# One PSUM tile of two banks for both halves of batch 0's kv, and the first half divided in two VectorE operations for four

## Chip, cores, metric

One core of one Trainium2 chip. The metric is the device time of an execution in microseconds (us). A time is the median of several runs unless a mean is named. The profile shows one execution each; its span is about 1.8 us shorter than the time.

## The reference, cut to what matters

Linear attention for 8 batches of 8 heads, 576 rows of 64, then a two-layer MLP with GELU on the result:

```python
q_s = softmax(q, axis=-1);  k_s = softmax(k, axis=2)      # k over the sequence
kv  = einsum('bhsd,bhse->bhde', k_s, v)                   # 64 x 64 for each head
x   = einsum('bhsd,bhde->bhse', q_s, kv)
out = gelu(x @ w_in) @ w_out                              # 4608 x 512, d_ff 2048
```

The kernel leaves out the division of k's softmax. It multiplies exp(k) by v with a column of ones added (65 columns), and divides kv by its 65th column afterwards.

## The kernel before

The MLP takes nearly all of the time on TensorE (lines 348, 376 and 401: 255.3 of its 270.9 us busy in the profile). The change touches the start-up, in which batch 0 is prepared while TensorE has nothing else to do.

```python
def kv_tiles(b):
    if b == 0:      # first half: two tiles of one bank; second half: a tile of two banks
        p = [psum_h.tile([128, 512], FP32, tag="h", name="kv")[:, 0:256] for i in range(2)]
        ps = psum_a.tile([128, 4, 256], FP32, tag="a2", name="kv")
        st[b]["kvall"] = ps[:, 0::2]
        p += [ps[:, 0, :], ps[:, 2, :]]
    else:           # other batches: all four pairs in one tile of two banks
        ps = psum_a.tile([128, 4, 256], FP32, tag="a2", name="kv")
        st[b]["kvall"] = ps
        p = [ps[:, i, :] for i in place]
    st[b]["kv"] = p
place = [1, 2, 0, 3]

# ... in kv_norm, for each part (src in PSUM, dst in SBUF, m pairs of heads):
    nc.vector.reciprocal(rec[:, 0:m], src[:, :, D])
    nc.vector.tensor_tensor(out=dst, in0=src[:, :, 0:D],
        in1=rec[:, 0:m].unsqueeze(2).to_broadcast([128, m, D]), op=ALU.mult)

# ... the start-up, in program order:
exp_q(0, parts=2)
exp_k(0, parts=2)
norm_q(0, 0, 2)                  # multiply on GpSimd (POOL)
norm_q(0, 1, 2, nc.vector)       # multiply on VectorE (DVE)
tp_mm(0, 0)                      # transposes of q for x of pairs 0, 1
cast_v(0, 0, nc.scalar)
cast_v(0, 1, nc.scalar)
tp_evac(0, 0)
cast_v(0, 2, nc.gpsimd)
cast_v(0, 3, nc.gpsimd)
# ... x tiles
tp_mm(0, 1)                      # transposes of q for x of pairs 2, 3
tp_evac(0, 1, "s")
# ...
kv_mm(0, 0)                      # kv of pairs 0, 1
kv_norm(0, 0)                    # their division
kv_mm(0, 1)                      # kv of pairs 2, 3
kv_norm(0, 1)
# ... casts of w_in, x tile
x_mm(0, 0); x_evac(0, 0, "s"); x_evac(0, 1)
x_mm(0, 1); x_evac(0, 2, "s"); x_evac(0, 3)
# ... then h_phase(0): the MLP
```

The softmax here doesn't subtract the row's maximum and nothing guards it: scores larger than these inputs give would overflow.

## Time and profile before

| | before |
|---|---|
| time | 279.40 us (3 runs, 279.39 to 279.44) |
| span of the profile | 277.5 us |
| TensorE busy | 98% |
| first half's division | 4 VectorE operations, 0.76 us from first start to last end |
| first MLP matmul | 13.97 us |

The row to watch is the last one. From there on TensorE (PE) runs without waits (busy 260.1 of the 263.5 us from 14 us to the end), so the time is the start of the MLP plus a constant.

### The profile page before, as it was taken

The numbers are of one execution on the slowest core, as the hardware profiler recorded it, in microseconds if no ns is written. First come the engines' busy times: TensorE is split into PE (matmuls) and PEld (weight loads), VectorE is DVE, ScalarE is ACT, GpSimd is POOL, SyncE is SP. The second block draws the span as 40 slices with busy tenths as digits, with TensorE's granted clock in tenths as the row PEclk, the third lists the DMA queues.
The fourth block names the chain that finished last, engine by engine and source line by source line (L and its number), as shares of the span: only waits on it lengthen the run. The fifth ranks groups of instructions, "written<-read, shape, count | busy, mean of one in ns | idle before, by whom it ended". The sixth has DMA issues, their size and how long they took to land.

```text
span 277.5 us, 4658 instructions
## 1 busy us (share of the span) xinstructions
PE 270.9 (98%) x1966; PEld 125.6 (45%) x1966; DVE 100.8 (36%) x154; ACT 158.9 (57%) x247; POOL 32.5 (12%) x26
## 2 busy tenths in 40 slices
PE   7799999999999999999999999999999999999995
PEld 3344454444444444444444444444444444444443
DVE  2876565319743540263008400751015200120012
ACT  4867686689377717791669246943683363126400
POOL 1520041002020310013000500050005000000000
PEclk9999999999999999999999999999999999999999
DMA  7999999974993249613981189117402500220033
GB/s 258 400 374 427 402 400 404 400 271 116 312 307 64 77 109 297 239 40 94 268 320 38 53 215 398 56 41 193 109 0 78 151 0 0 78 76 0 2 76 77
DMA packets 44980, 50.10 MB, mean 181 GB/s; under 512 B 20384, under 2 KB 29856, under 8 KB 44704
## 3 DMA queue, kind: packets, MB, share of 16 engines
q1 hardware_dynamic: 44560, 49.39, 53.5%
q10 hardware_dynamic: 400, 0.43, 0.5%
q8 instruction: 15, 0.25, 0.4%
q14 instruction: 5, 0.04, 0.1%
HBM read 36.70 MB, written 9.44 MB: 166 GB/s over the span
## 4 chain that ended last, share of the span: by engine, by line
PE 94%; DMA 4%; POOL 0%; DVE 0%; issue 0%; SPq 0%
PE ps L348 44%; PE ps L376 44%; DMA f<-in_v_dram 2%; PE kv L206 2%; PE ps L315 2%; DMA f<-in_q_dram 2%; PE ps L401 1%; PE pair L348 1%; POOL v_aug L169 0%; PE ps L320 0%; PE tp L279 0%; SPq L103 0%; DVE kvc L225 0%; DVE y_sb L406 0%; DVE rec L224 0%
## 5 line engine op out<-in xcount | busy, mean ns | idle before, releaser
L348 PE MATMUL ps<-xT,wi_bf 128*128 128x512 bf16 x568 | 124.9, 379 | 0.0
L376 PE MATMUL ps<-wo_bf,g 128*128 128x512 bf16 x560 | 124.1, 379 | 0.0
L354 ACT ACTIVATE g<-ps 128x512 bf16<-128x512 f32 x142 | 83.5, 598 | 66.8 <-PE ps L348 66.7
L348 PEld LDWEIGHTS <-wi_bf 128*128 128x128 bf16 x576 | 56.2, 98 | 68.0 <-issue 0.8
L376 PEld LDWEIGHTS <-g 128*128 128x128 bf16 x560 | 54.0, 98 | 64.6 <-issue 0.4
L384 DVE COPY y_sb<-ps 128x512 f32<-128x512 f32 x33 | 22.7, 687 | 81.0 <-PE ps L376 80.7
L245 POOL TENSOR_TENSOR e<-e,recq 128x2048 bf16<-128x2048 bf16 (+1 forms) x9 | 25.7, 2855 | 175.9 <-DVE recq L244 141.2
L169 DVE CAST v_aug<-f 128x576 bf16<-128x576 f32 x24 | 16.4, 746 | 48.3 <-DMA f<-in_v_dram 48.3
L243 DVE TENSOR_REDUCE qsum<-e 128x16 f32<-128x1024 bf16 (+1 forms) x13 | 21.1, 1622 | 13.7 <-ACT e L152 13.6
L341 ACT CAST xT<-ps 128x512 bf16<-128x512 f32 x18 | 9.9, 588 | 26.4 <-PE ps L315 15.9
L152 ACT ACTIVATE e<-f 128x512 bf16<-128x512 f32 (+1 forms) x42 | 20.5, 556 | 3.5 <-DMA f<-in_q_dram 3.5
L157 ACT ACTIVATE ek<-f 128x2304 bf16<-128x2304 f32 (+1 forms) x10 | 17.2, 1728 | 0.6 <-DMA f<-in_k_dram 0.5
L339 DVE CAST xT<-ps 128x512 bf16<-128x512 f32 x17 | 11.0, 687 | 17.1 <-PE ps L315 14.1
L79 ACT ACT_TABLE_LOAD x9 | 11.5, 1283 | 2.8 <-issue 2.7
L494 PE MATMUL ps<-zeros 128*128 128x512 f32 x14 | 8.0, 734 | 1.5 <-DVE zeros L520 1.5
L152 ACT ACT_TABLE_LOAD x7 | 9.0, 1283 | 0.1
L453 DVE CAST wi_bf<-w 128x512 bf16<-128x512 f32 x12 | 7.1, 621 | 1.8 <-DMA w<-in_moe_w_in_dram 1.4
L206 PEld LDWEIGHTS <-ek 64*64 64x64 bf16 x576 | 6.4, 105 | 2.2 <-issue 0.6
L206 PE MATMUL kv<-v_aug,ek 64*64 64x65 bf16 x576 | 6.8, 193 | 0.5 <-POOL v_aug L169 0.5
L487 DVE CAST wo_bf<-w 128x2048 bf16<-128x2048 f32 (+1 forms) x5 | 4.5, 907 | 6.1 <-DMA w<-in_moe_w_out_dram 6.1
L245 DVE TENSOR_TENSOR e<-e,recq 128x1024 bf16<-128x1024 bf16 x4 | 6.2, 1544 | 0.1
L315 PE MATMUL ps<-qT,kvc 64*64 64x512 bf16 x62 | 5.4, 390 | 0.3 <-DVE kvc L225 0.3
(40 smaller groups left out, 48.2 us busy)
## 6 DMA issues: line engine op xcount, KB each, us to landing
out_dram<-y_sb SPq DMA_DIRECT2D x32, 256.0 KB, 2.4
f<-in_k_dram SPq DMA_DIRECT2D x6, 1152.0 KB, 9.9
f<-in_v_dram SPq DMA_DIRECT2D x6, 1152.0 KB, 11.7
f<-in_q_dram SPq DMA_DIRECT2D x6, 1024.0 KB, 7.7
w<-in_moe_w_in_dram SPq DMA_DIRECT2D x6, 512.0 KB, 8.6
f<-in_v_dram SPq DMA_DIRECT2D x8, 288.0 KB, 6.5
f<-in_q_dram SPq DMA_DIRECT2D x4, 512.0 KB, 8.9
w<-in_moe_w_out_dram SPq DMA_DIRECT2D x2, 1024.0 KB, 11.4
```

What stands on the lines that cost most here:

```text
L79: nc.scalar.activation(out=scr[:, 1:2], in_=scr[:, 0:1], func=func)
L152: nc.scalar.activation(out=dst[:, i], in_=src[:, u], func=AF.Exp)
L157: nc.scalar.activation(out=ek[b % 2][:, i:i + n], in_=st[b]["kf"][:, i:i + n].rearrange("p x (n d) -> p x n d", n=NS), func=AF.Exp,)
L169: eng.tensor_copy(out=o, in_=i)
L206: nc.tensor.matmul(st[b]["kv"][hp][c, 0:D + 1], ek[b % 2][pr, hp, n, :], v_aug[b % 2][pr, hp, n, 0:D + 1], start=(n == 0), stop=(n == NS - 1),
L243: nc.vector.reduce_sum(out=qsum, in_=eq[:, :, hs, :], axis=AX.X)
L245: eng.tensor_tensor(out=eq[:, :, hs, :], in0=eq[:, :, hs, :], in1=recq.unsqueeze(3).to_broadcast([128, J, w, D]), op=ALU.mult,)
L339: nc.vector.tensor_copy(out=st[b]["xT"][:, hp, :], in_=ps)
L348: nc.tensor.matmul(ps, wi_bf[:, dm, t * 128:(t + 1) * 128], st[c]["xT"][:, dm, :], start=(dm == 0), stop=(dm == NDM - 1),)
L354: nc.scalar.activation(out=st[c]["g"][:, t, :], in_=ps, func=AF.Gelu)
L376: nc.tensor.matmul(ps, st[c]["g"][:, t, j * 128:(j + 1) * 128], wo_bf[:, t, :], start=(t == 0), stop=(t == NDF - 1),)
L384: nc.vector.tensor_copy(out=y_sb, in_=ps)
```

## The change

Its intent is to treat batch 0 as the other batches are treated: kv of all four pairs in one PSUM tile of two banks. Pairs 0 and 1 then lie side by side, so that one reciprocal and one multiply divide both. Two VectorE operations fewer, and two PSUM buffers fewer taken.

```diff
     def kv_tiles(b):
-        if b == 0:
-            p = [psum_h.tile([128, 512], FP32, tag="h", name="kv")[:, 0:256] for i in range(2)]
-            ps = psum_a.tile([128, 4, 256], FP32, tag="a2", name="kv")
-            st[b]["kvall"] = ps[:, 0::2]
-            p += [ps[:, 0, :], ps[:, 2, :]]
-        else:
-            ps = psum_a.tile([128, 4, 256], FP32, tag="a2", name="kv")
-            st[b]["kvall"] = ps
-            p = [ps[:, i, :] for i in place]
-        st[b]["kv"] = p
+        ps = psum_a.tile([128, 4, 256], FP32, tag="a2", name="kv")
+        st[b]["kvall"] = ps
+        st[b]["kv"] = [ps[:, i, :] for i in place]
 ...
-        elif b == 0 and half == 0:
-            parts = [(st[b]["kv"][hp].unsqueeze(1), kvc[b][:, hp:hp + 1], 1) for hp in range(2)]
-        elif b == 0:
-            parts = [(ps, kvc[b][:, 2:4], 2)]
         else:
             parts = [(ps[:, 1:3] if half == 0 else ps[:, 0::3], kvc[b][:, 2 * half:2 * half + 2], 2)]
```

## The prediction

> **What bounds the kernel now.** I read the page's first part, then the waits of PE, then the chain that ended last, and at last the timeline of the two microseconds that the change touches.
>
> ```profile
> PE 270.9 (98%) x1966; PEld 125.6 (45%) x1966; DVE 100.8 (36%) x154; ACT 158.9 (57%) x247; POOL 32.5 (12%) x26
> ```
>
> TensorE (PE) is busy 98% of a span of 277.5 us; VectorE (DVE), whose instructions the change cuts from 154 to 152, only 36%. Busy is not proof, so who stops PE? The list of PE's waits, over the whole span:
>
> ```profile
> PE ps L494 <- DVE zeros L520: 1.5, 1, 1.5
> PE ps L259 <- DVE e L245: 0.6, 1, 0.6
> PE kv L206 <- POOL v_aug L169: 0.5, 1, 0.5
> PE ps L259 <- POOL e L245: 0.4, 1, 0.4
> PE ps L315 <- DVE kvc L225: 0.3, 1, 0.3
> ```
>
> Columns: who waited, for whom, us in total, times, longest. Asked again from 14 us on, the list holds only the last line (that wait began before 14). So after the start-up PE never waits by this view; anything that moves the start of the dense part moves the end, one for one. All that matters is what sets the moment, 13.97 us, at which the first MLP matmul (line 348) starts. The chain of waits between 10 and 16 us (start, length, what):
>
> ```profile
> 11.12 0.67 POOL v_aug L169
> 11.79 0.05 issue
> 11.83 0.68 POOL v_aug L169
> 12.51 0.04 issue
> 12.55 0.50 PE kv L206 x34
> 13.05 0.02 issue
> 13.08 0.18 DVE rec L224
> 13.26 0.02 issue
> 13.28 0.30 DVE kvc L225
> 13.58 0.04 issue
> 13.63 0.41 PE ps L315 x4
> ```
>
> This chain is of batch 0's **second** half: v arrives, GpSimd (POOL) casts two slices, PE makes kv of head pairs 2 and 3, DVE divides them (one reciprocal, one multiply), PE makes x of pairs 2 and 3. The four DVE operations of the **first** half, which the change merges, are not in it. The timeline shows them beside it:
>
> ```profile
> 12.08 0.17 DVE L224 RECIPROCAL rec<-kv 128x1 f32<-128x1 f32 x1 [0.61 <-PE kv L206]
> 12.28 0.23 DVE L225 TENSOR_TENSOR kvc<-kv,rec 128x64 bf16<-128x64 f32 x1
> 12.42 0.16 DVE L224 RECIPROCAL rec<-kv 128x1 f32<-128x1 f32 x1
> 12.55 0.47 PE L206 MATMUL kv<-v_aug,ek 64*64 64x65 bf16 x34 [0.50 <-POOL v_aug L169]
> 12.61 0.23 DVE L225 TENSOR_TENSOR kvc<-kv,rec 128x64 bf16<-128x64 f32 x1
> 13.08 0.17 DVE L224 RECIPROCAL rec<-kv 128x2 f32<-128x2 f32 x1 [0.24 <-PE kv L206]
> 13.28 0.29 DVE L225 TENSOR_TENSOR kvc<-kv,rec 128x128 bf16<-128x128 f32 x1
> ```
>
> PE starts kv of the second half at 12.55, in the middle of these four: today it does not wait for them, because they read other PSUM tiles than it writes. This is the point on which my prediction rests.
>
> [...] In the new tile of two banks, pair 0 lies in slot 1 and pair 2 in slot 0 of the same bank, pairs 1 and 3 in the other: the second half's matmuls write the banks that the first half's division reads. [...] The built program agrees: against the kernel before, PE's list has exactly one new wait, on VectorE at the first weight load of kv's second half, and lacks three: the two on VectorE ahead of the first x matmuls (now covered by the earlier one) and one on an earlier PE result. No other wait differs. [...]
>
> [...] 64 columns more take a multiply from 0.226 to 0.291 us (65 ns, about 1 ns a column), and a reciprocal of 2 columns takes 0.171 against 0.157 to 0.169 for 1. So merging pays on DVE; the question is only who waits.
>
> **The change part by part.** Starts below are of single records in the trace, in us.
>
> 1. DVE. Before: reciprocal 12.076, multiply 12.279, reciprocal 12.421, multiply 12.612, the last ends at 12.838; 0.762 from start to end. After: one reciprocal and one multiply of the forms that the second half shows (13.076, then 13.281 for 0.291: 0.496 from start to end). Saved on DVE: 0.762 - 0.496 = 0.27 us; the division ends at 12.076 + 0.496 = 12.572 instead of 12.838.
>
> 2. What this gain could free. Next in PE's queue behind kv's second half is x of pairs 0 and 1. PE works in order and issues its last kv matmul at 12.838; the x matmul of pair 0 went at 12.841, that of pair 1 at 12.893, because the division ended at 12.838 and a weight load follows its DVE signal after about 0.053 (12.838 to 12.891; again 13.572 to 13.624). So at most 0.05 us, and in x of the first half, whose only follower is an ACT copy of xT that ends at 13.924.
>
> 3. The new wait. kv's second half starts now 0.052 after the POOL cast (12.501 to 12.553). After: 12.572 + 0.053 = 12.625, when the cast is long ready. Cost: 12.625 - 12.553 = 0.072 us, on the chain. Two of its 36 matmuls, which went ahead at 11.86 before, now come after the wait. The 36 of the first half took 0.289 from first to last start (11.549 to 11.838) against 0.285 for the 34 (12.553 to 12.838): 0.004 more.
>
> 4. From there the chain moves as a whole: last kv matmul 12.914, reciprocal 0.238 later, multiply 0.205 later, x of pairs 2 and 3 0.343 after that: 13.70 instead of 13.626. DVE was free from 12.838 and idle 0.24 us before the second half's reciprocal, so its saved work helps nothing here.
>
> 5. The first MLP matmul, before at 13.974, had two things to meet: PE's own switch after the last x matmul (13.636 + 0.332, the gap that the same switch shows at 44.637 to 44.969) = 13.968, and xT of pair 0, ended at 13.924 plus 0.05 = 13.974. After: the first is 13.713 + 0.332 = 14.045; the second, with x of the first half starting about 12.917 without a wait for pair 1, ends its copy near 13.953, so 14.003. The larger sets it: 14.045 - 13.974 = **0.07 us later**.
>
> 6. PSUM buffers. The two tiles no longer taken from the three-buffer pool advance its rotation by two. x of pair 3 gets a fresh bank instead of one used by a transpose; the next MLP tiles still find one that was freed long ago. Worth: 0, as the list of waits says.
>
> 7. Downstream. Between 14 and 39.6 us no matmul starts more than 0.25 after the one before, so no cast or load now stops PE, and being later only adds slack. The larger gaps later (0.31 to 0.41, around 40 and 44 us, and one or two per batch) are switches of matrix shape and an ACT copy that PE itself releases; they move along. Nothing absorbs the 0.07.
>
> Sum: +0.07 us on 279.40, so **279.47 us**, +0.03%.
>
> **The rivals.**
> - *The division is on the path, and two operations fewer bring a gain.* For it: PE's list has a wait for kvc at line 315. Against it: the chain shows that this is the second half's division, which is already two operations. It could give 0.05 to 0.27: 279.1 to 279.35.
> - *The wait is hidden anyway*: if the division ended before the POOL cast, or if the shift met slack at 13.97. The margin is small: the cast is ready at 12.501 and the division at 12.572. A reciprocal starting 0.07 earlier, or v landing 0.07 later in a run, makes it 0: 279.40. Half hidden is quite possible[...].
> - *The wait costs more than I count*: the semaphore covers a later operation, or weight loads that ran ahead before the cast was ready now queue behind the wait. That would add about 0.1 (a weight load takes 0.103): 279.6. Against: at line 315 a load behind a DVE signal and its matmul start within 0.002.
> - *The shift pushes transfers*: the cast of wi part 1 on DVE (14.72) frees a staging buffer and moves 0.07 later; but the queue sets out one load every 0.6 us or more and PE has no wait on these data. 0.
>
> **Range and chances.** All mechanisms together lie within -0.3 and +0.2 us. The three runs of before span 0.05 us, but its profiled run took 279.26, so another session may move by about 0.15. Range 279.2 to 279.75. Two per cent is 5.6 us, more than the whole stage from 11.1 to 14: within 2% is all but certain, 0.98. What is left goes slightly more to slower[...]: 0.013, faster 0.007.
>
> **What would show it.** In the profile after: two DVE operations for the first half, 128x2 and 128x128, ending 0.50 after their start; kv's second half starting about 0.05 after that end with VectorE named in place of POOL, near 12.62; both x groups and the first line-348 matmul about 0.07 later; PE's total unchanged. Wrong would be: kv's second half still beginning before the division ends (then the wait is not what I read), POOL still named as its releaser, the first MLP matmul at 13.97 or earlier, or a time below 279.3 or above 279.7 in paired runs.

The sum came to +0.07 us on 279.40, so 279.47 us.

## The result, and the profile after

| | before | after |
|---|---|---|
| time | 279.39 us (6 runs, 279.25 to 279.44) | 279.62 us (6 runs, 279.54 to 279.76) |
| ratio of the fast runs | | 1.0009, interval 0.9997 to 1.0022 |
| span of the profile | 277.5 us | 277.9 us |
| VectorE busy, instructions | 100.8 us, 154 | 100.0 us, 152 |
| first MLP matmul | 13.97 us | 14.33 us |

A ratio is the mean time of one kernel's fast runs over that of the other's of the same rounds, so not quite the ratio of the medians quoted. Within 2%, as predicted. The interval even holds 1.0, but no run of after is as fast as any of before, and a second session (below) gave +0.21 us again, though there some runs of the two overlap. So I take the change to be slower by about 0.2 us.

The list of PE's waits after the change (who, for whom, us in total, times, longest):

```profile
PE ps L483 <- DVE zeros L509: 1.5, 1, 1.5
PE ps L248 <- POOL e L234: 0.7, 1, 0.7
PE kv L199 <- DVE kvc L214: 0.6, 1, 0.6
PE ps L248 <- DVE e L234: 0.5, 1, 0.5
PE ps L304 <- DVE kvc L214: 0.4, 1, 0.4
```

Behind the edit, line numbers are 7 or 11 lower. The third line is new: kv now waits for VectorE's kvc, where it waited for POOL's cast of v. The timeline of the same stage (start, length, engine, operation, and in brackets the idle time before it and what ended it):

```profile
10.97 1.37 POOL L169 CAST v_aug<-f 128x576 bf16<-128x576 f32 x2 [0.93 <-DMA f<-in_v_dram]
...
12.35 0.17 DVE L213 RECIPROCAL rec<-kv 128x2 f32<-128x2 f32 x1 [0.63 <-PE kv L199]
12.55 0.29 DVE L214 TENSOR_TENSOR kvc<-kv,rec 128x128 bf16<-128x128 f32 x1
12.89 0.37 PEld L199 LDWEIGHTS <-ek 64*64 64x64 bf16 x36 [0.73 <-DVE kvc L214]
12.90 0.48 PE L199 MATMUL kv<-v_aug,ek 64*64 64x65 bf16 x36 [0.61 <-DVE kvc L214]
```

The merged division works as meant: two operations, 0.50 us. But PE starts the second half only behind them, at 12.90, although POOL had v cast at 12.34. What now stands behind this moment is seen in the chain of waits:

```profile
9.40 1.73 DVE e L234
11.13 0.14 issue
11.27 0.61 PE ps L248 x8
11.87 0.45 PE kv L199 x36
12.32 0.02 issue
12.35 0.18 DVE rec L213
12.53 0.02 issue
12.55 0.30 DVE kvc L214
12.85 0.04 issue
12.90 0.52 PE kv L199 x35
```

Before, v's transfer and casts led to kv's second half. After, it is the q path: normalization, transposes, kv's first half, its division. In this run that path is also later than in the profile before (transposes at 11.27, not 11.01), for a reason that nothing in the change explains at once. Whether that is chance was the first question to test.

### The profile page after: what moved, and what is told of

The parts are those of the page before. It is cut to its first block, busy times and chain, and to the rows that moved or that the text cites. A ratio compares the mean times of both kernels' runs of the same rounds, so it can differ in the third digit from the quotient of the medians.

```text
span 277.9 us, 4656 instructions
## 1 busy us (share of the span) xinstructions
PE 270.7 (97%) x1966; PEld 125.5 (45%) x1966; DVE 100.0 (36%) x152; ACT 158.7 (57%) x247; POOL 32.4 (12%) x26
## 4 chain that ended last, share of the span: by engine, by line
PE 94%; DVE 2%; DMA 2%; ACT 0%; issue 0%
PE ps L337 44%; PE ps L365 44%; PE kv L199 2%; DMA f<-in_q_dram 2%; PE ps L304 2%; PE ps L390 1%; DVE qsum L232 1%; DVE e L234 1%; PE pair L337 1%; ACT e L152 0%; PE ps L309 0%; PE tp L268 0%; PE ps L248 0%; DVE kvc L214 0%; DVE recq L233 0%
```

## The experiments

All results are correct, and all runs used are of granted clock 0.998 to 1.000. Times are against the kernel before in the same session (each session ran on another chip). Two names help. **V** is the end of POOL's last v cast plus 0.05 us. **K** is the last kv matmul of the first half plus 0.79 (0.24 to the reciprocal, 0.50 for the division, 0.05 to PE), from the profile before. In kernels that merge or share, the reciprocal starts 0.25 to 0.26 behind that matmul, so that 0.81 is nearer. Theory A says that kv's second half starts at V before the change, and at the later of V and K after it.

### Session 1: again, without the shared banks, without the merging

**Before again, after again**: unchanged kernels.

> The kernel before, unchanged, as a control and for a second profile. Theory A (bank wait: kv's second half now starts at the later of two moments, V = POOL's last v cast + 0.05, and K = last kv matmul of the first half + 0.79, and the difference K - V varies from run to run): time 1.000 within 0.05 us; kv's second half names POOL as its releaser; K - V computed from the records, 0.07 in the first profile, comes out different by 0.1 or more. Rival B (the 0.25 us by which the q path was late in the profile after belongs to the changed program): here the last transposes start within 0.05 of 11.01 and the DVE multiply of e takes about 1.5 again.

> The changed kernel again. Theory A: +0.15 to +0.30 us over before; in the profile kv's second half starts 0.32 to 0.34 after the multiply of the first half starts (0.29 + 0.05), VectorE named; the start of the transposes moves by 0.1 or more against the first profile after (11.27), in either direction. Rival B: the transposes start at 11.27 within 0.05 again and the multiply of e takes 1.72 again.

**Merged, in banks of its own**: the first half in a separate two-bank tile; the warm-up matmuls, x of pairs 0 and 1 and three MLP tiles take other buffers for it. Core of the edit against after:

```diff
         st[b]["kv"] = [ps[:, i, :] for i in place]
+        if b == 0:
+            st[b]["kv01"] = psum_t.tile([128, 4, 256], FP32, tag="t", name="kv")
+            st[b]["kv"][:2] = [st[b]["kv01"][:, i, :] for i in place[:2]]
 ...
-        ps = st[b]["kvall"]
+        ps = st[b]["kv01"] if b == 0 and half == 0 else st[b]["kvall"]
```

> Two operations for the first half, as in the change, but the first half's kv in a tile of two banks of its own (x of pairs 0 and 1 takes other buffers for that), so that kv's second half writes no bank that the division reads. Theory A: no wait on VectorE, POOL named, time as before: 0.00 within 0.10 us. Rival B (merged operations or the new buffer rotation cost the time by themselves): +0.2 us as after. Rival C (the saved 0.27 us of VectorE is worth something where no wait is in its way): -0.05 to -0.25 us.

**Shared tile, four operations**, against after:

```diff
+        elif b == 0 and half == 0:
+            parts = [(ps[:, 1 + hp:2 + hp], kvc[b][:, hp:hp + 1], 1) for hp in range(2)]
         else:
```

> The tile of the change, but the first half divided by four operations as before. Theory A: the wait lasts to the end of the fourth, 0.27 us later than with two, all on the chain: +0.27 over after, +0.45 to +0.55 us over before. Rival B (the shared tile costs by slower access or by rotation, not by the wait for the division): as after, within 0.05 us.

| kernel (5 runs; before 279.38, 9 runs) | time | against before |
|---|---|---|
| before again | 279.36 | -0.02 |
| after again | 279.59 | +0.21 |
| merged, own banks | 279.27 | -0.11 |
| shared, four operations | 279.72 | +0.34 |

With the banks apart, the same two operations cost nothing; they gain a tenth, if anything (the ratio is 0.9997, and its interval holds 1.0). POOL is named again, and PE starts while the multiply still runs:

```profile
12.18 0.17 DVE L217 RECIPROCAL rec<-kv 128x2 f32<-128x2 f32 x1 [0.48 <-PE kv L203]
12.39 0.29 DVE L218 TENSOR_TENSOR kvc<-kv,rec 128x128 bf16<-128x128 f32 x1
12.54 0.48 PE L203 MATMUL kv<-v_aug,ek 64*64 64x65 bf16 x34 [0.39 <-POOL v_aug L170]
```

With the tile shared and four operations, PE waits to the end of the fourth:

```profile
12.79 0.22 DVE L216 TENSOR_TENSOR kvc<-kv,rec 128x64 bf16<-128x64 f32 x1
13.07 0.37 PEld L199 LDWEIGHTS <-ek 64*64 64x64 bf16 x36 [0.99 <-DVE kvc L216]
```

So the loss comes with the shared tile and not with the merging. (The runs do not separate sharing a tile from sharing its two banks: own banks changes both.) In the records, kv's second half starts 1.07 us after the last kv matmul of the first half here, and 0.81 in both profiles of after: the 0.27 expected, within 0.01. The time shows only half of that or less (+0.13 between the two medians, +0.06 between the means, as one run of after again took 280.03). That was a miss in size.

Before again had K - V = 0.14 (0.07 in the first profile), after again 0.24 and after 0.51: it varies from run to run, by q and by v alike (over the six profiles so far L, the last kv matmul of the first half, spans 0.29 us and the end of the last cast 0.27). Between the two profiles of before it moved by only 0.07, where I had expected 0.1 or more, and their transposes (11.01 and 10.98) lie as close together as rival B said. But those of after again began at 11.08, not 11.27, so rival B's fixed 0.25 us is refuted. A smaller fixed part is not.

### Session 2: take the q path out; make v late

**kv first**, in both kernels: kv of pairs 0 and 1 doesn't need q at all. It only stood behind the second transposes in PE's queue.

```diff
+    kv_mm(0, 0)
+    kv_norm(0, 0)
     tp_mm(0, 1)
     tp_evac(0, 1, "s")
     x_tile(0, 2, psum_a, "a")
-    kv_mm(0, 0)
-    kv_norm(0, 0)
```

> The changed kernel, with kv's first half and its division issued ahead of the second set of q transposes (which only x of pairs 2 and 3 needs), so that kv's first half no longer waits for the normalization of q. Theory A (the cost is the wait, and its size is set by how late the q path makes kv's first half): kv's first half starts near 11.3 instead of 11.55 to 11.8, its division ends near 12.3, before POOL's cast, the wait is there but finds its signal given; POOL is named again; time as before or up to 0.1 faster, that is 0.2 to 0.3 us faster than after. Rival D (the shared banks cost by something else than how long that wait lasts): still +0.2 us over before.

> The kernel before with the same reordering. Theory A: the kernel before is held by v in most executions and by the q path (first half's division, x, copy of xT) in others, so a little is gained, 0.0 to -0.1 us; the difference from after_kv_first is below 0.05 us. Rival D: 0.2 us apart from after_kv_first.

**v late**, in both kernels, a POOL copy that nobody reads:

```diff
+    nc.gpsimd.tensor_copy(out=pad, in_=zeros32[:, 0:256])
     cast_v(0, 3, nc.gpsimd)
```

> The kernel before with a useless POOL copy of 128x256 (0.36 us from start to start in the profile) between the last two casts of v. Theory A: V moves by 0.36, and the time by +0.25 to +0.36 us, for in this kernel v is what holds kv's second half.

> The changed kernel with the same useless POOL copy. Theory A: V now comes later than K in most executions, the wait is hidden, POOL is named; the time is within 0.08 us of before_v_late, so about +0.3 over before and only +0.1 over after. Rival D (a cost of the shared banks that does not depend on who comes last): +0.2 us over before_v_late, +0.5 over before.

| kernel (5 runs; before 279.41, 9 runs) | time | against before |
|---|---|---|
| after, kv first | 279.24 | -0.17 |
| before, kv first | 279.16 | -0.25 |
| before, v late | 279.50 | +0.09 |
| after, v late | 279.61 | +0.20 |

One reordering takes the changed kernel from +0.2 to -0.17. Both are now faster than the kernel before by a little: no run of either is above 279.31 and none of before below 279.37, though the intervals of the ratios (0.9979 to 1.0005 and 0.9976 to 1.0001) still hold 1.0. I had expected less (0.0 to -0.1), since I still thought that v held the kernel before in most runs. And the two were to lie within 0.05 us of each other; they lie 0.08 apart (0.09 between the means), so a small cost of the change is left here that theory A does not give. In the changed kernel the division ends at 12.09, ahead of POOL's cast (12.29):

```profile
11.80 0.29 DVE L214 TENSOR_TENSOR kvc<-kv,rec 128x128 bf16<-128x128 f32 x1
...
12.14 0.68 PE L199 MATMUL kv<-v_aug,ek 64*64 64x65 bf16 x36
```

My expectation that POOL would be named was only half met: the first two matmuls, of pair 2, start behind the division, and the next, of pair 3, waits for the cast (12.34).

The gain of 0.22 us at the first MLP matmul (13.76 against 13.97) did not all reach the end. PE's weight loads, in the same kernel's list of waits, now wait three times for the casts of w_in:

```profile
PEld L337 <- DVE wi_bf L442: 0.9, 3, 0.4
```

The last of these costs PE 0.14 us at 24.9 us. Its cast ends at 24.86; these casts follow the transfer of w_in (in the page of before, 1.4 of the 1.8 us of VectorE's idle time ahead of them is put down to it). This suggests a floor just below the time before; it is read from one profile. In before with kv first, whose MLP starts at 13.91, no such gap is to be seen.

The v-late pair was inconclusive: before with v late came out at +0.09, not +0.25 to +0.36, and the two lie 0.11 apart (0.02 between the means). V moved by only 0.2 to 0.3 us, as part of the copy fell into POOL's wait for the transfer (in the profile of before the last slice of v landed at 11.782, just as the cast ahead ended at 11.785, and the last cast started at 11.834; in before with v late the copy started at 11.72, 0.05 before the cast ahead ended), and in the profile of after with v late K was still the later one (12.92 against 12.67).

### Session 3: make one path surely the last

**q late**, in both: a VectorE memset that nobody reads, in the normalization of q's first half.

```diff
         nc.vector.reduce_sum(out=qsum, in_=eq[:, :, hs, :], axis=AX.X)
+        if b == 0 and i == 0:
+            nc.vector.memset(pad, 0.0)
```

> The kernel before with a useless VectorE memset of 128x512 (0.485 us in the profile) between the sum and the reciprocal of the first half of q, so that the normalization of q, and with it kv's first half, is about 0.47 later. By the records of the eight profiles so far the first MLP matmul starts in this kernel at the later of V + 1.42 and (last kv matmul of the first half) + 2.14, and these two tie in normal runs, so +0.4 to +0.5 us over before.

> The changed kernel with the same memset. Here the first MLP matmul starts at (last kv matmul of the first half) + 2.23. Theory A (only the wait): with q surely the last in both kernels the difference from before_q_late is the difference of the two chains, 0.09 us (0.05 to 0.13). Rival E (the changed program also gets q later, by the 0.1 to 0.18 us by which its profiles differ so far): the difference is 0.2 or more.

**v last**, in both: two POOL copies instead of one.

> The kernel before with two useless POOL copies instead of one (the single copy moved V by less than 0.36 because part of it fell in POOL's wait for the transfer). V near 13.1: +0.5 to +0.7 us over before; POOL named.

> The changed kernel with the same two copies: K (12.6 to 12.9 so far) is now surely earlier than V, so the wait for the division is over when the cast ends. Theory A: POOL named ahead of the matmuls on pair 3; within 0.05 us of before_v_last. Rival D (the shared banks cost in any case): +0.2 us over before_v_last.

| kernel (5 runs; before 279.50, 9 runs) | time | mean against before |
|---|---|---|
| before, q late | 279.75 | +0.22 |
| after, q late | 279.92 | +0.39 |
| before, v last | 279.83 | +0.34 |
| after, v last | 279.79 | +0.33 |

The padding cost before less than I had expected (+0.4 to +0.5 with q late, +0.5 to +0.7 with v last). I had reckoned from the profiles of before, and these are of two of its fastest runs (279.26 and 279.20), with an early q: against the first of them the first MLP matmul is later by 0.50 and 0.58. Also, the memset moved L by 0.36 only, from 6.89 to 7.25 us after the first exp of q.

With v surely last the cost of the change is gone: 0.00 between the means (and -0.04 between the medians; the five runs of both span 279.7 to 280.06). The timeline of after with v last shows both waits, one behind the other, the first of them harmless:

```profile
12.50 0.29 DVE L215 TENSOR_TENSOR kvc<-kv,rec 128x128 bf16<-128x128 f32 x1
...
12.84 0.22 PE L200 MATMUL kv<-v_aug,ek 64*64 64x65 bf16 x2 [0.61 <-DVE kvc L215]
13.23 0.47 PE L200 MATMUL kv<-v_aug,ek 64*64 64x65 bf16 x34 [0.17 <-POOL v_aug L170]
```

This refutes rival D as stated (shared banks cost 0.2 us in any case). With q last, the kernel **before** is held by q too. Its kv matmuls form one group of 72 without a wait named, and PE waits instead for the copy of xT, behind the first half's division and x:

```profile
PE ps L351 <- ACT xT L344: 0.3, 1, 0.3
```

In the two q-late profiles the first half's first reciprocal starts at the same moment (12.580), and their first MLP matmuls lie at 14.478 and 14.564. That is 0.086, as theory A has it (0.09). The time says 0.17, between theory A and rival E. Starts in us of single records, for the runs that the argument uses (L: last kv matmul of the first half; division: its end; v: end of the last cast; kv2: first kv matmul of the second half, in after with v last that of pair 3):

| profile | first exp of q | L | division | v | kv2 | first MLP matmul | span |
|---|---|---|---|---|---|---|---|
| before | 4.95 | 11.838 | 12.838 | 12.501 | 12.553 | 13.974 | 277.5 |
| before again | 4.92 | 11.804 | 12.802 | 12.398 | 12.451 | 13.939 | 277.4 |
| merged, own banks | 5.04 | 11.928 | 12.678 | 12.488 | 12.540 | 13.954 | 277.4 |
| after | 5.20 | 12.091 | 12.843 | 12.335 | 12.897 | 14.334 | 277.9 |
| after again | 5.02 | 11.908 | 12.659 | 12.425 | 12.715 | 14.153 | 277.7 |
| shared, four | 5.11 | 11.999 | 13.013 | 12.601 | 13.068 | 14.506 | 278.0 |
| before, q late | 5.09 | 12.341 | 13.341 | 12.500 | 12.552 | 14.478 | 278.0 |
| after, q late | 5.07 | 12.325 | 13.074 | 12.484 | 13.128 | 14.564 | 278.1 |
| before, v last | 5.13 | 12.026 | 13.023 | 13.089 | 13.141 | 14.553 | 278.0 |
| after, v last | 5.15 | 12.037 | 12.788 | 13.179 | 13.232 | 14.648 | 278.2 |

Span minus first MLP matmul is 263.5 to 263.6 in all of these: what happens in the start-up reaches the end unchanged. Before the change, the first MLP matmul comes at the later of kv2 + 1.42 (1.41 with v last) and division + 1.14. After it, it comes at kv2 + 1.44 (1.42 in the last row, where pair 2's matmuls had gone ahead), and kv2 is the later of L + 0.81 and v + 0.05 (L + 1.07 with four operations).

## Why the prediction was right, and where not

**PE bounds the kernel, and a later start of the MLP is a later end**: right; 263.5 us from there to the end in both kernels. What I left out is that the reverse doesn't hold: starting 0.22 earlier met the weights of w_in.

**The new wait** (step 3): right in its form. kv's second half starts 0.054 after the division ends (12.843 to 12.897), where I had taken 0.053. Session 1 shows that it is the shared tile, with its banks, that brings it, and session 3 that it costs nothing once v comes last.

**Its size**: this is the step that was off. The term was "12.625 - 12.553 = 0.072 us". Both moments were read off one profile and treated as fixed; I allowed for v's transfer to vary, not for q's. K - V was 0.07 and 0.14 in the profiles of before, 0.51 and 0.24 in those of after. The timed cost was 0.23 and 0.21 us instead of 0.07, about three times as much. A small term was also missing: the merged reciprocal needs both pairs and starts 0.255 behind the last kv matmul, where I kept the 0.238 of the first of four. That 279.62 lies in my range is due to the range, not to the sum. The third rival named 279.6, but by luck: its weight loads that queue behind the wait are not there, as the first load starts 0.052 after the division.

**"What this gain could free: at most 0.05"** (step 2) and the first rival's dismissal ("the chain shows that this is the second half's division"): too firm. In step 5 I saw two chains meet within 0.006 us at the first MLP matmul, and did not ask what a faster first half would do to the one that runs through its division. That one was clearly the later in before again (12.802 + 1.14 = 13.94, against 12.451 + 1.42 = 13.87). So the merging has some worth, the tenth that the own-banks version may show, and the shared tile more than takes it back. The profile that I worked from misled me here: its run took 279.26. As the rest of a run is constant, a run of 279.40 starts its MLP near 14.11 (an estimate: 13.974 + 0.14). The latest v cast without padding in any profile (12.60) gives at most 14.07 by the rules above, while L of 11.97 gives 14.11, and L was 11.80 to 12.09. And if v held it, kv first would have had nothing to gain. So the kernel before is probably held by q, and with it by the first half's division, in most runs; no run shows it directly.

**PSUM rotation and downstream transfers** (steps 6 and 7) worth nothing: nothing contradicts it.

**What stays open.** By the table's rules, the same L and v give the changed kernel at most (L + 0.81 + 1.44) - (L + 1.00 + 1.14) = 0.11 us more, 1.00 being the time from L to the end of four operations. The timed 0.21 to 0.23 contains 0.1 more. In the profiles it appears as a q path that is later in after (first exp of q 5.20 and 5.02) than in before (4.95 and 4.92). But kernels that share the tile had 5.07 to 5.22, and kernels that don't had 4.99 to 5.24 when other edits were made to them. Over all 14 profiles the mean is 5.12 with the shared tile and 5.05 without, within spreads of 0.20 and 0.32. So I can't say whether the changed program gets its q later or the few profiles happened to fall so. Four operations in the shared tile costing 0.13 more than two, rather than 0.27, and the 0.08 that is left with kv first may belong to the same gap. It needs many profiles of the two unchanged programs.

## What to carry to other kernels

Putting data into one PSUM tile in order to merge operations here also shared the tile's waits: kv's second half started 0.054 us after the end of the first half's division in after, and 0.138 before it in merged, own banks. In after, 0.81 us passed from the last kv matmul of the first half to the first of the second: 0.255 to the reciprocal, 0.497 for the division, 0.054 to PE. Where v came last (after, v last) this cost nothing against before, v last. So before saving an instruction, look at which writer of the same tile must now stand behind the reader. Where a wait is the later of two moments that both hang on transfers, one profile gives the margin of one run only; take several, or make each path late in turn, as with q late and v last here. And when two chains meet within hundredths of a microsecond, neither is "not on the path". Work that needs nothing from a late input should also not stand behind it in an engine's queue: moving kv's first half up gave about 0.25 us in the kernel before, as much as the change lost.

## What the runs showed that I had not expected

VectorE's multiply of q's second half took between 1.38 and 1.74 us, and in all 14 profiles it ended 1.08 us after POOL's multiply of the first half (1.079 to 1.082), however early it began. It looks as if it got on only when POOL's was done; no run shows the cause. In these runs the whole q path follows the arrival of q's **first** half: L lies 6.89 us after the first exp of q (6.888 to 6.893) in all six unpadded profiles with the original order, although q's second half comes 1.4 to 1.7 us after the first.
